# Other PSUM banks for the second product and the third channel block, and one chunk's sums in float32

## The chip, the cores and the metric

The kernel runs on one core of a Trainium2 chip. The metric is the device time of one execution in microseconds (us), the median over the runs shown. Beside it there is one profiled execution, whose trace is read here. The engines are TensorE (PE for matmuls, PEld for the loads of the stationary operand), VectorE (DVE), ScalarE (ACT), GpSimd (POOL) and SyncE (SP, which issues most transfers). Matmuls write to PSUM, which has eight banks of 512 float32 columns on 128 partitions.

## The reference

Two blocks follow one another. The first is a gated linear recurrence over 4 batches, 8 heads, 768 steps and head size 48; the second is a mixture of 8 experts, of which each row takes the best one.

```python
for t in range(S):                                   # recurrence, per batch and head
    state = alpha[:, :, t, :, None] * state + einsum('bhd,bhe->bhde', k[:, :, t], v[:, :, t])
    y[:, :, t] = einsum('bhd,bhde->bhe', q[:, :, t], state)
x = y.transpose(0, 2, 1, 3).reshape(3072, 384)
expert_idx = argmax(x @ w_gate, axis=1)              # w_gate 384 x 8
for e in range(8):                                   # w1[e] 384 x 1024, w2[e] 1024 x 384
    rows = (expert_idx == e)
    out[rows] = gate_w[rows] * (relu(x[rows] @ w1[e]) @ w2[e])
```

gate_w is the softmax weight of the chosen expert. All is float32.

## The kernel before

The instructions of every engine are issued in the order in which the program writes them (a manual schedule); the framework adds the waits that the tiles' readers and writers ask for.

**Recurrence.** The 3072 steps are 24 chunks of 128, taken in the order chunk s = 4 * (time block) + batch. The loop at line 720 runs over i; step i does the scores of chunk i, the transposes of chunk i + 1, the operands of chunk i + 2, the output rows of chunk i - 1 and the running sums of log alpha for chunks up to i + 5 (functions `sums_to` and `new_sums`, lines 619 to 623). A running sum is a matmul of a triangular matrix with the logarithms of 128 steps (`cums`, line 431); ACT then takes two exponentials from the bank `cum` (lines 440 and 441). There are two forms. In the plain one the matmul is float32 (line 434; a float32 product stands in the trace as two loads and two matmuls). In the split one (`apart`, line 411: chunk 7 and chunks from 11 on) ACT makes a float16 copy of the logarithms (line 422), DVE the remainder (`low_part`, line 427), and PE does one float16 and one float32r matmul (lines 436 and 437). The sums of chunks 6 and 7 are both made in step i = 2; chunk 7's is the second, after `attend` and ahead of `keys_values` in PE's order, and its `low_part` stands between the two copies of `transposes` (line 488).

**Experts.** Rows are sorted to eight places by expert size; each place is one group of up to 424, 416, ... 368 rows. 256 rows of place 0 are computed early (`early_layer1` beside the end of the recurrence; `early_layer2`, line 1207, for their second product, in two blocks j = 0 and 1, of which j = 1 is done in two parts with the first product of the other rows of place 0 between them). Places 1 to 7 use a Strassen-like scheme with seven block products (`chain`, line 903; `layer1`, line 952; `layer2`, line 1020): p1 to p7, each in a PSUM bank taken in turn from a pair. Products p1, p3, p5, p6 use pair pA, p4 and p7 pair pB, and p2, the "second product", pair pC. In `layer2` the scheme makes output channels 0 to 255; the third channels (256 to 383) are a plain product of eight float32 matmuls into `d2` (lines 1051 to 1062), whose bank comes from pair pC as well, straight after p2. So p2 of layer 2 writes one bank of pC and `d2` the other. The result of p2 is taken out by a DVE addition into zT (line 924 through the helper at line 192), and `d2` by an ACT copy (line 1064).

**Banks.** `bank(n)` (line 846) hands out the two banks of a pair alternately. pA is the tiles sA and x, pB cum and sB, and tp two tiles of the name tp. pC is the two halves of `y`, which is one tile of two banks: it held outputs and states of the recurrence.

**Turning.** Gathered rows of places 0 and 1 are transposed on PE (`turn`, line 862), block by block of 128 rows, three transposes each; even blocks are copied out by DVE and odd ones by ACT. Place 0 has two blocks here and place 1 four (the last of 32 rows). All four of place 1 alternate between the two tp banks. From place 2 on the transposing is done by transfers (`x_halves`, `x_whole`).

Of the kernel before, what the change touches and what calls it, by code (L numbers as in the profile page):

```python
# [8 lines left out]
F32 = mybir.dt.float32  # L9
# [11 lines left out]
def kernel(  # L21
# [31 lines left out]
    C = 128  # L53
# [180 lines left out]
    g0 = groups[0]  # L234
# [154 lines left out]
    with tc.tile_pool(name="ld", bufs=6) as ld, \  # L389
# [18 lines left out]
            for i in range(many):  # L408
                st[s + i][n] = t[:, i]

        def apart(s):

            return s >= APART or s == 7

        def logs(s):
            t = work.tile([C, Dm], F32, name="lna", bufs=4)
            nc.scalar.activation(t[:], st[s]["a"].rearrange("s h d -> s (h d)"), AF.Ln)
            st[s]["lna"] = t
            if apart(s):

                st[s]["hi"] = work.tile([C, Dm], F16, name="hi", bufs=2)
                nc.scalar.mul(st[s]["hi"][:], t[:], HS)

        def low_part(s):

            t = st[s]["lo"] = work.tile([C, Dm], F32R, name="lo", bufs=1)
            nc.vector.scalar_tensor_tensor(
                t[:], in0=st[s]["hi"][:], scalar=-1.0 / HS, in1=st[s]["lna"][:], op0=ALU.mult, op1=ALU.add,
            )

        def cums(s, bank="cum"):
            cum = ps.tile([C, 512], F32, name="cum", tag=bank)
            if not apart(s):
                nc.tensor.matmul(cum[:, :Dm], lhsT=cum_m[:], rhs=st[s]["lna"][:], start=True, stop=True)
            else:
                nc.tensor.matmul(cum[:, :Dm], lhsT=cum_h[:], rhs=st[s]["hi"][:], start=True, stop=False)
                nc.tensor.matmul(cum[:, :Dm], lhsT=cum_r[:], rhs=st[s]["lo"][:], start=False, stop=True)
            cp = work.tile([C, Dm], F32, name="cp", bufs=6)
            icp = work.tile([C, Dm], F32, name="icp", bufs=6)
            nc.scalar.activation(icp[:], cum[:, :Dm], AF.Exp, scale=-1.0)  # L440
            nc.scalar.activation(cp[:], cum[:, :Dm], AF.Exp)
            st[s]["cp"], st[s]["icp"] = cp, icp
# [42 lines left out]
                    d[e][:].rearrange("s (a p d) -> s a p d", a=2, p=NP), op=ALU.mult,  # L485
                )

        def transposes(s, *lows):
            d = st[s]
            for i, n in enumerate(("kT", "qT")):  # L490
                if i:
                    for t in lows:
                        low_part(t)
                tp = ps.tile([C, NP, C], F32, name="tp", bufs=2)
                for p in range(NP):
                    nc.tensor.transpose(tp[:, p, :], pair(kqb[s % 3][:, i], p), ident[:])  # L496
                d[n] = work.tile([C, NP, C], F32, name=n)

                if 0 < s < B - 1 or i and s < NT - B - 2:
                    nc.vector.tensor_copy(d[n][:], tp[:])  # L500
                else:
                    nc.scalar.copy(d[n][:], tp[:])  # L502
# [217 lines left out]
        for i in range(-4, NT):  # L720
            loads_for(i)
            do(scores, i)
            if i < NT - 1:
                do(result, i - 1)
            do(logits, i - 2)
            if i >= B:
                do(add_state, i - 1)
            do(gate, i - 2)
            if i > 0:
                for s in new_logs(i):  # L730
                    logs(s)
            if 0 < i < NT and i % B == 0:
                decay_cols(i // B)
            do(mask, i, 0)
            do(mask, i, 1)
            if i < B:
                do(add_state, i - 1)
            do(transposes, i + 1, *[s for s in new_sums(i) if apart(s) and s < APART])
            sums = list(new_sums(i))
            for s in sums[:1]:  # L740
                cums(s)
            if i < 0:
                for s in sums[1:]:
                    cums(s, "x")
            do(gate_weight, i - 2)
            route(i)
            for s in new_logs(i):
                if s >= APART:
                    low_part(s)
            do(keep_rows, i - 2)  # L750
            if len(sums) == 1:
                decay_out(sums[0])
            if i == -1:
                for s in range(2):
                    decay_out(s)

            if B - 1 <= i < 2 * B - 1:
                decay_out(i + 1, (1,))
            if i == NT - 2:
                si = next(se)[1]  # L760
                eg["si"] = lambda j, r: si[:r, j : j + 1]
            if i in (B, 2 * B):
                scale_state(i)
            do(operands, i + 2)
            if i > 2 * B and i % B == 0:
                scale_state(i)
            if 0 < i + 1 < NT and (i + 1) % B == 0:
                decay_rows((i + 1) // B)
            elif i >= 0:
                do(scale_state, i + 1)  # L770
            one_hots(nc.gpsimd, *on_gpsimd.get(i, ()))
            do(read_state, i)
            if i == NT - 1:
                early_turn(0)
            do(attend, i)
            if i == NT - 1:
                early_turn(1)
            if i == NT - 2:
                result(i)
            if i >= 0 and sums[1:]:  # L780
                cums(sums[1])
                for s in sums:
                    decay_out(s, (0,) if i else (0, 1))
            do(keys_values, i)
            if i == NT - 3:
                held["tok"] = ps.tile([C, NC], F32, name="tok", tag="cum")
                tokens(held["tok"][:], *range((NG - 1) * TG))
                se = early_gather()
            do(rows, i - 1)
            if i in counts_in:  # L790
                counts(counts_in[i], counted(i - 1))
            if i < 0:
                for s in new_sums(i + 1):
                    logs(s)
            if i == -3:
                second_consts()
            if i in (-4, 0, 1):
                for j in {-4: (0, 1, 2), 0: (3,), 1: (4,)}[i]:
                    late_consts(j)
            if 12 <= i < 22:  # L800
                fetch_part(groups[0], i - 12)
# [38 lines left out]
    xg_pool = ctx.enter_context(tc.tile_pool(name="moe_x", bufs=2))  # L840
    wk = ctx.enter_context(tc.tile_pool(name="moe_wk", bufs=1))

    pairs = dict(pA=("sA", "x"), pB=("cum", "sB"), pC=(0, 1), tp=("tp", "tp"))
    banks = {n: [] for n in pairs}

    def bank(n):
        b = banks[n]
        if len(b) < 2:
            t = pairs[n][len(b)]
            if n == "pC":  # L850
                b.append(y[:, t, :])
            else:
                b.append(ps.tile([C, 512], F32, name=t, bufs=2 if n == "tp" else 1)[:])
        else:
            b.append(b.pop(0))
        return b[-1]
# [2 lines left out]
        return t[:, : DB * C].rearrange("p (a c) -> p a c", a=DB)  # L859


    def turn(g, second="tp"):
        g["xT"] = wk.tile([C, DB, CAP0 + 8], F32, name="xgT")
        for j, r in blocks(g):
            tp = blocks_of(bank(second if j == 1 else "tp"))
            for a in range(DB):
                nc.tensor.transpose(tp[:, a, :r], g["xg"][:r, j, a * C : (a + 1) * C], ident[:r, :r])
            (nc.scalar.copy if j % 2 else nc.vector.tensor_copy)(g["xT"][:, :, j * C : j * C + r], tp[:, :, :r])
            if j == 1:
                yield  # L870
# [336 lines left out]
    def early_layer2(j, fs):  # L1207

        if 0 in fs:
            eg["z"] = bank("tp" if j else "pA")  # L1210
        for f in fs:
            nc.tensor.matmul(
                eg["z"][:, :Dm], lhsT=eg["h"][:, f, j * C : (j + 1) * C], rhs=groups[0]["w2"][:, f, :],
                start=(f == 0), stop=(f == FB - 1),
            )
        if FB - 1 in fs:
            yield
            scatter(eg, j, C, eg["z"][:, :Dm])
        yield
# [35 lines left out]
    gather(groups[1])  # L1255
    next(l2)
    next(early_layer2(1, range(FH)))
    for _ in turn(g0, "pC"):
        pass

    def beside(i):
# [8 lines left out]
    for i, g in enumerate(groups):  # L1270
# [36 lines left out]

        def turned():
            if i == 0:
                for _ in turn(nxt):  # L1310
                    pass
                yield
                row_sums(nxt)
                yield
            z_whole(groups[i - 1], nc.scalar.copy, 0, 1)
            yield
            if nxt:
                row_sums(nxt)
            z_whole(groups[i - 1], nc.scalar.copy, 2)
            z_whole(groups[i - 1], nc.vector.tensor_copy, 3)  # L1320
            yield
            if i + 2 < E:
                for _ in x_halves(groups[i + 2]):
                    pass
            yield
# [25 lines left out]
    with tc.If(nx > 0):  # L1351
        with tc.For_i(0, nx, 1) as i:
# [12 lines left out]
            gi, si = next(d)[:2]  # L1365
            g = dict(n=C, w1=fetch(ex, 1), w2=fetch(ex, 2), gi=lambda j, r: gi[:, 0:1], si=lambda j, r: si[:, 0:1], apart=False)
            gather(g)
            for _ in turn(g):
                pass
            plain(g)  # L1370

# [27 lines left out]
```

## Time and profile before

| | |
|---|---|
| median of 3 runs | 400.71 us (400.21 to 401.31) |
| profiled execution | 401.6 us |
| its span on the core | 399.9 us |
| granted TensorE clock | 0.999 |
| PE busy | 384.2 us, 96% of the span |
| PEld busy | 325.5 us, 81% |
| ACT, DVE, POOL busy | 225.1, 215.4, 147.9 us |

A profile line names an engine, a line of the code, an operation, and the tiles written and read (`y<-h_sb,w` writes y and reads h_sb and w). Where an engine stood idle before an instruction, brackets give for how long and whose end released it. The end of a matmul is modelled, so two consecutive matmuls overlap in the records. The stages of the span are roughly: recurrence to 136 us, place 0 to 177 us, places 1 to 6 to 364 us (some 32 us each), and place 7 to the end.

### The profile page before, as it was taken

The page shows a single profiled execution, that of the slowest core. Times are in us where ns is not written, and L with a number is a line of the kernel's source. Part 1 is how long each engine was busy: PE and PEld are TensorE (multiplying, and loading weights), DVE is VectorE, ACT ScalarE, POOL GpSimd, SP SyncE. Part 2 cuts the span into 40 slices and gives each one's busy share as a digit, 9 for nine tenths or more (in the row PEclk, how much of TensorE's full clock was granted, in tenths as well). Part 3 has the DMA queues.
Part 4 walks back from the last instruction along what each step waited for, and adds up shares of the span by engine and source line. Part 5 has one row for each costly group of instructions (what it writes and reads, how often), then busy time and mean ns, then how long its engine had stood idle before and what let it go on. Part 6 is the DMA issues. An engine that isn't in the chain of part 4 may idle for free.

```text
span 399.9 us, 9108 instructions
## 1 busy us (share of the span) xinstructions
PE 384.2 (96%) x3390; PEld 325.5 (81%) x3390; DVE 215.4 (54%) x652; ACT 225.1 (56%) x516; POOL 147.9 (37%) x203
## 2 busy tenths in 40 slices
PE   7999999999999999999999999999999999999994
PEld 4677888888888886799789879969969969969852
DVE  5554667775666574586833662572591581551200
ACT  4575677776655431125565765665665755763640
POOL 6536564699677105182050034025015012011041
PEclk9999999999999999999999999999999999999999
DMA  8999999999994218769739449758757856701311
GB/s 162 194 185 201 204 216 202 218 222 219 234 227 156 79 41 282 259 177 247 164 93 254 72 195 216 158 179 221 158 190 197 182 179 143 188 6 55 59 57 55
DMA packets 153921, 67.44 MB, mean 169 GB/s; under 512 B 136715, under 2 KB 148098, under 8 KB 153876
## 3 DMA queue, kind: packets, MB, share of 16 engines
q1 hardware_dynamic: 148772, 57.13, 59.7%
q0 software_dynamic: 3408, 9.64, 7.9%
q8 instruction: 27, 0.44, 0.4%
q10 hardware_dynamic: 1696, 0.08, 0.3%
q14 instruction: 18, 0.15, 0.1%
HBM read 49.00 MB, written 9.58 MB: 147 GB/s over the span
## 4 chain that ended last, share of the span: by engine, by line
PE 67%; issue 15%; DMA 4%; ACT 3%; DVE 3%; POOL 3%; SPq 2%; ACTq 1%; POOLq 0%; DVEq 0%
PE y L1055 7%; PE sA L509 4%; PE tp L496 4%; PE y L546 4%; PE x L973 4%; PE sA L973 4%; PE sA L1038 4%; PE x L583 3%; PE y L973 3%; PE cum L973 3%; PE sB L973 3%; PE x L1038 3%; DMA q_sb<-in_q_dram 3%; PE y L536 2%; SPq L405 2%
## 5 line engine op out<-in xcount | busy, mean ns | idle before, releaser
L1085 POOL DMA_INDIRECT out_dram<-zo,sp x25 | 24.8, 991 | 143.2 <-ACT zo L1110 132.2
L1055 PE MATMUL y<-h_sb,w 128*128 128x416 f32 (+5 forms) x96 | 34.5, 502 | 3.7 <-DVE zT L192 3.7
L483 POOL TENSOR_TENSOR kqb<-k_sb,icp 128x384 f32<-128x384 f32 x23 | 23.0, 998 | 30.9 <-DMA k_sb<-in_k_dram 15.9
L1055 PEld LDWEIGHTS y<-h_sb,w 128*128 128x128 f32 x96 | 17.6, 190 | 15.8 <-DVE zT L192 5.5
L509 PE MATMUL sA<-qT,kT 48*128 48x128 f32 x192 | 27.7, 285 | 0.9 <-DVE qT L500 0.9
L509 PE MATMUL sB<-qT,kT 48*128 48x128 f32 x192 | 27.7, 285 | 0.0
L372 POOL DMA_INDIRECT xg<-x_rows,gp x25 | 23.9, 957 | 10.0 <-issue 6.5
L496 PE MATMUL tp<-ident,kqb 128*128 128x128 f32 x192 | 26.2, 280 | 0.2 <-DVE kqb L483 0.2
L509 PEld LDWEIGHTS sA<-qT,kT 48*128 48x128 f32 x192 | 23.1, 187 | 3.8 <-ACT kT L502 1.1
L565 ACT COPY yT<-y 128x512 f32<-128x512 f32 x24 | 14.1, 586 | 19.1 <-PE x L583 9.8
L192 DVE TENSOR_TENSOR h_sb<-cum,u 128x208 f32<-128x208 f32 (+6 forms) x28 | 10.1, 359 | 27.3 <-PE cum L973 20.8
L483 POOL TENSOR_TENSOR kqb<-q_sb,cp 128x384 f32<-128x384 f32 x23 | 23.0, 1001 | 4.1 <-DMA q_sb<-in_q_dram 2.8
L984 ACT ACTIVATE h_sb<-h_sb 128x208 f32<-128x208 f32 (+6 forms) x28 | 10.3, 366 | 25.2 <-DVE h_sb L192 24.4
L192 DVE TENSOR_TENSOR h_sb<-sB,u 128x208 f32<-128x208 f32 (+6 forms) x28 | 10.1, 359 | 26.1 <-PE sB L973 18.7
L496 PEld LDWEIGHTS tp<-ident,kqb 128*128 128x128 f32 x192 | 20.6, 141 | 3.4 <-issue 1.1
L973 PE MATMUL y<-xgT,w 128*128 128x208 f32 (+6 forms) x112 | 23.1, 329 | 0.0
L509 PEld LDWEIGHTS sB<-qT,kT 48*128 48x128 f32 x192 | 23.1, 187 | 0.0
L517 DVE TENSOR_TENSOR dA<-sA,cmask 128x512 f32<-128x512 f32 x24 | 16.5, 687 | 10.1 <-PE sB L509 9.9
L195 DVE TENSOR_TENSOR th<-h_sb,th 128x208 f32<-128x208 f32 (+5 forms) x48 | 17.3, 361 | 7.9 <-ACT h_sb L986 7.9
L583 PE MATMUL x<-iw,yT 128*64 128x104 f32 x368 | 20.8, 255 | 0.3 <-ACT xs L608 0.2
L1110 ACT COPY zo<-zr 128x768 uint16<-128x768 uint16 (+2 forms) x20 | 19.9, 1052 | 0.0
L973 PEld LDWEIGHTS y<-xgT,w 128*128 128x128 f32 x112 | 19.2, 190 | 0.0
(305 smaller groups left out, 1034.0 us busy)
## 6 DMA issues: line engine op xcount, KB each, us to landing
w<-in_moe_w_dram SPq DMA_DIRECT2D x14, 1536.0 KB, 6.4
x_rows<-xs SPq DMA_DIRECT2D x24, 192.0 KB, 3.6
v_sb<-in_v_dram SPq DMA_DIRECT2D x10, 384.0 KB, 5.4
k_sb<-in_k_dram SPq DMA_DIRECT2D x9, 384.0 KB, 6.6
q_sb<-in_q_dram SPq DMA_DIRECT2D x9, 384.0 KB, 5.9
a_sb<-in_alpha_dram SPq DMA_DIRECT2D x7, 384.0 KB, 4.9
a_sb<-in_alpha_dram SPq DMA_DIRECT2D x10, 192.0 KB, 3.8
w<-in_moe_w_dram SPq DMA_DIRECT2D x6, 256.0 KB, 4.0
```

The costliest lines, as they stand in the source:

```text
L192: eng.tensor_tensor(out, a, b, op=ALU.add)
L195: eng.tensor_tensor(out, a, b, op=ALU.subtract)
L372: nc.gpsimd.indirect_dma_start(out=g["xg"][:r, j, :], out_offset=None, in_=x_d[:, :], in_offset=bass.IndirectOffsetOnAxis(ap=g["gi"](j, r) ...
L483: eng.tensor_tensor(by_half(kq[:, i]), d[n].rearrange("s (a p) d -> s a p d", a=2), d[e][:].rearrange("s (a p d) -> s a p d", a=2, p=NP), ...
L496: nc.tensor.transpose(tp[:, p, :], pair(kqb[s % 3][:, i], p), ident[:])
L509: nc.tensor.matmul(t[:, p, :], lhsT=d["kT"][r : r + D, p, :], rhs=d["qT"][r : r + D, p, :], start=True, stop=True,)
L583: nc.tensor.matmul(d["x"][o : o + HC, m, : D2 + E], lhsT=d["yT"][:, m // 2, m % 2, o : o + HC], rhs=iw[:, m, :], start=True, stop=True,)
L973: nc.tensor.matmul(out, lhsT=ops[n_][0], rhs=ops[n_][1], start=first and n_ == names[0], stop=True, skip_group_check=True,)
L1038: nc.tensor.matmul(out, lhsT=lhs, rhs=rhs, start=first and f == 0, stop=True, skip_group_check=True)
L1055: nc.tensor.matmul(d2[:, :n], lhsT=w2[:, f, 2 * C :], rhs=h[:, f, :n], start=(f == 0), stop=(f == FB - 1),)
L1085: ins = nc.gpsimd.indirect_dma_start(out=out[:, :], out_offset=bass.IndirectOffsetOnAxis(ap=g["si"](j, r), axis=0), in_=zo[:r], in_offset= ...
L1110: copy(zo[:r].bitcast(U16).rearrange("p (c h) -> p h c", h=2), g["zr"][:r, j].rearrange("p (h a) c -> p h (a c)", h=2),)
```

## The change

Three edits stand together.

1. pC becomes the two tiles called tp, and the halves of `y` become a pair of their own, named y. All uses of pC (p2 in both layers, `d2`, the first product of place 0, the first row block of place 7) move with it.
2. The early second product of block 1 takes a bank of y in place of tp. `turn` takes a list of pair names, one for each block: place 0's two blocks use pC (tp); place 1's four blocks use pC, pC, y and pB, so four different banks.
3. Chunk 7 is no longer split: its sum is the plain float32 matmul, with no float16 copy on ACT and no remainder on DVE. The extra argument of `transposes` goes.

```diff
-        def apart(s):
-            return s >= APART or s == 7
...
-            if apart(s):
+            if s >= APART:
...
-            if not apart(s):
+            if s < APART:
...
-        def transposes(s, *lows):
+        def transposes(s):
...
-                if i:
-                    for t in lows:
-                        low_part(t)
...
-            do(transposes, i + 1, *[s for s in new_sums(i) if apart(s) and s < APART])
+            do(transposes, i + 1)
...
-    pairs = dict(pA=("sA", "x"), pB=("cum", "sB"), pC=(0, 1), tp=("tp", "tp"))
+    pairs = dict(pA=("sA", "x"), pB=("cum", "sB"), pC=("tp", "tp"), y=(0, 1))
...
-            if n == "pC":
+            if n == "y":
                 b.append(y[:, t, :])
             else:
-                b.append(ps.tile([C, 512], F32, name=t, bufs=2 if n == "tp" else 1)[:])
+                b.append(ps.tile([C, 512], F32, name=t, bufs=2 if t == "tp" else 1)[:])
...
-    def turn(g, second="tp"):
+    def turn(g, *names):
...
-            tp = blocks_of(bank(second if j == 1 else "tp"))
+            tp = blocks_of(bank(names[j]))
...
-            eg["z"] = bank("tp" if j else "pA")
+            eg["z"] = bank("y" if j else "pA")
...
-    for _ in turn(g0, "pC"):
+    for _ in turn(g0, "pC", "pC"):
...
-                for _ in turn(nxt):
+                for _ in turn(nxt, "pC", "pC", "y", "pB"):
...
-            for _ in turn(g):
+            for _ in turn(g, "y"):
```

The last line belongs to a loop over rows beyond a group's capacity. It follows the end of the chain described here and its bank choice changes nothing else.

## The prediction

> **What bounds the kernel now.** I read first the busy times and the shares of the chain that ended last, to learn which engine a saving must come from.
>
> ```profile
> PE 384.2 (96%) x3390; PEld 325.5 (81%) x3390; DVE 215.4 (54%) x652; ACT 225.1 (56%) x516; POOL 147.9 (37%) x203
> ...
> PE 67%; issue 15%; DMA 4%; ACT 3%; DVE 3%; POOL 3%; SPq 2%; ACTq 1%; POOLq 0%; DVEq 0%
> ```
>
> PE is busy all through and carries most of the chain; no other engine reaches 60%. So in the expert stages a PE pause removed should be worth its length, and one added costs its length. The view of waits then names PE's own pauses; the longest in total, on the loads and on the matmuls (columns: total us, times, longest):
>
> ```profile
> PEld y L1055 <- DVE zT L192: 5.5, 6, 1.0
> ...
> PE y L1055 <- DVE zT L192: 3.7, 6, 0.6
> ```
>
> Six times, once in each of places 1 to 6, the third channels (line 1055) wait for a DVE addition into zT. The timeline of place 1 shows which:
>
> ```profile
> 195.78 0.30 PEld L1038 LDWEIGHTS y<-h_sb,w 128*128 128x128 f32 x2 [0.32 <-ACT h_sb L986]
> ...
> 196.62 0.37 DVE L192 TENSOR_TENSOR zT<-y,p 128x208 f32<-128x208 f32 x1
> ...
> 197.04 0.30 PEld L1055 LDWEIGHTS y<-h_sb,w 128*128 128x128 f32 x2 [0.97 <-DVE zT L192]
> 197.04 3.06 PE L1055 MATMUL y<-h_sb,w 128*128 128x416 f32 x8 [0.65 <-DVE zT L192]
> ```
>
> The last loads of p2 start at 195.78; the addition that empties p2's bank ends at 196.99; only then does the first matmul of d2 start. But d2 writes the other bank of pC, last emptied in layer 1 some 6 us earlier, and zT is none of its operands. The one thing both share is the tile y. So the wait is kept by tile, and d2 pays for p2's evacuation.
>
> Place 1's turning is the next PE pause, in the timeline at 167 us:
>
> ```profile
> 167.67 0.48 ACT L1081 COPY zo<-tp 128x384 f32<-128x384 f32 x1 [3.12 <-PE tp L1212]
> ...
> 168.21 0.87 PE L867 MATMUL tp<-ident,xg 128*128 128x128 f32 x6 [0.57 <-ACT zo L1081]
> ...
> 168.86 0.56 DVE L868 COPY xgT<-tp 128x384 f32<-128x384 f32 x1 [3.42 <-PE tp L867]
> ...
> 169.47 0.85 PE L867 MATMUL tp<-ident,xg 128*128 128x128 f32 x6 [0.39 <-DVE xgT L868]
> ...
> 170.25 2.55 PE L1243 MATMUL x<-h_sb,w 128*128 128x168 f32 x16
> ```
>
> Block 0 waits until the early product has left its tp bank (ACT), block 2 until block 0 has left it (DVE). Last, the split sum of chunk 7 against a plain one:
>
> ```profile
> 18.34 0.91 PE L434 MATMUL cum<-lna,cum_m 128*128 128x384 f32 x2
> ...
> 19.18 0.56 PE L557 MATMUL y<-v_sb,kqb 128*48 128x48 f32 x16
> ...
> 23.04 0.52 ACT L422 ACTIVATE hi<-lna 128x384 f16<-128x384 f32 x1
> ...
> 23.59 0.56 DVE L427 SCALAR_TENSOR_TENSOR lo<-hi,lna 128x384 fp32r<-128x384 f16 x1 [0.44 <-ACT hi L422]
> ...
> 24.31 0.49 ACT L441 ACTIVATE cp<-cum 128x384 f32<-128x384 f32 x1
> ...
> 24.86 0.32 PE L436 MATMUL cum<-hi,cum_h 128*128 128x384 f16 x1 [0.57 <-ACT cp L441]
> ...
> 24.88 0.47 PE L437 MATMUL cum<-lo,cum_r 128*128 128x384 f32 x1
> ...
> 25.28 0.56 PE L557 MATMUL y<-v_sb,kqb 128*48 128x48 f32 x16
> ```
>
> From a sum's start to the next product, plain takes 19.18 - 18.34 = 0.84 us of PE, split 25.28 - 24.86 = 0.42. The chain in order of time says what binds there:
>
> ```profile
> 20.18 3.89 DMA k_sb<-in_k_dram
> ...
> 24.71 5.72 DMA q_sb<-in_q_dram
> ```
>
> Loads of k and q, not PE, set the pace until about 31 us.
>
> **What the Trainium skill says.** "PSUM — Partial Sum Buffer", section "PSUM bank collisions raise a hardware error": two engines must be kept apart on one bank, while accesses to different banks run clean. So nothing in the chip orders d2 behind p2's evacuation; the trace's 0.9 us is the program's. "Perfetto Trace Analysis", section "Matmuls", asks for independent matmul groups to rotate through banks so that one's evacuation overlaps the next's matmuls: the trace shows the opposite at 197 us. The same page, "Tensor Engine Instruction (MATMUL, LD_WEIGHTS)", says that a matmul's end is estimated. It fits: the records of consecutive matmuls overlap here, so I size stalls from the starts of loads.
>
> **Part 1, pC as two tiles.** In place 1 p2's last two loads start at 195.78, the second 0.11 later, as after any pause; at 0.176 us per 208-column matmul PE is free for d2 at about 196.24. It got d2's first matmul at about 197.14 (eight at 0.347 plus a tail of 0.18 end at 200.10). That is 0.91 lost, against 0.97 shown on the load row. The total of that row less 0.06 for each restart: 5.5 - 6 x 0.06 = 5.2 us over six places. Nothing takes the wait's place: d2's rhs (blocks 0 to 3 of h) is written by 194.29, w2 landed long before, and with six uses of pC per place d2's new bank was last emptied by layer 1's fourth addition (189.75 + 0.36).
>
> Does the gain stay? Behind d2, p6 needs a DVE difference that ends at 196.14, and would start at 199.03. DVE's sums for the next place end at 203.57 and layer 1 starts at 209.59: 6 us of cover, 5 after the shift. ACT's four xgT copies end at 198.70, ahead of the copy of p6 at 201.60, which moves to 200.7. Weights, gathers and transposes are issued a place ahead (32 us), so 0.9 us each, 5 in all, does not reach them. All else moves with PE. p2 in layer 1 gains nothing: its earlier addition is always done. Place 7 has no d2, and its rows show no such wait. I take -5.2, with 0 and -5.5 as ends.
>
> **Part 2, place 1's turning.** The early product ends on PE at about 167.46 (its record minus the 0.17 overlap). Blocks 0 and 1 go to tp banks last emptied at 164.6, so start at once: 6 transposes at 0.107 = 0.64, to 168.1. Block 2 goes to the second half of y, whose first half the ACT copy of the early product reads until 168.15: by tile it waits until 168.20, 0.1 us. Blocks 2 and 3 then take as now 170.25 - 169.47 = 0.78, and line 1243 starts at 168.98 for 170.25: -1.27. If block 2 need not wait, -1.4; if the earlier start is given back before place 1, 0. Given back means a wait at 177.05, where layer 1 starts: it needs xT (ready before 170), s1 and t1. DVE makes these after the turning copies, so earlier too; its 3.13 us subtraction at 174.04, which runs beside POOL's copies, would be done before POOL's first one at 174.58. Place 0's two blocks wait for their gather as before (0).
>
> **Part 3, chunk 7.** ACT loses 0.52, DVE 0.56, PE gains work of 0.42. The sum waits for the bank cum, freed by ACT's cp (24.80); with ACT 0.5 earlier it starts at 24.34 and lasts 0.84, so keys_values starts at 25.18 for 25.28: -0.1. Behind it stand PE's rows and the next scores, and ACT's exponentials of chunk 7, 0.2 earlier. All is covered by the loads until 31 us. Without that cover it costs at most 0.42. I take 0, ends -0.5 (ACT's lead kept) and +0.42.
>
> **Sum.** -5.2 - 1.27 + 0 = -6.5 on the profiled 401.6 us (span 399.9 plus 1.7 around it): 395.1. The median of the runs lies 0.9 below the profiled one: 400.7 - 6.5 = 394.2.
>
> **Rivals.**
> *The wait isn't by tile.* If d2 waits for another reason, only part 2 is left: 399.4. Against it: six equal waits that end 0.05 us after the addition. Chance 0.06.
> *Given back.* ACT or DVE becomes what PE waits for in places 1 to 6, where PE already waits 0.3 to 0.4 us for ACT copies (line 915). Half of part 1 lost: 396.8. Against it: 5 us of cover. Chance 0.07.
> *Nothing.* As the last, and part 2 lost with part 1: 400.7. Chance 0.03.
> *Slower: the clock.* PE gets busier; a throttle would lower the granted clock. It is 0.999 now; the stretch from 170 to 366 us, about half the run, would have to fall to about 0.97 for PE's 190 us there to lose 6.5. At 0.95 the time is 394.2 + 10 = 404. For it nothing shows. Against it: the clock row is all nines, in slices with PE at 9 too. Chance 0.06.
>
> **How the numbers follow.** The likeliest case (0.78) lies at 394.2, with ends 392.9 to 395.9. The range 392.6 to 397.0 takes in "given back" and leaves out about 2 in 10 with the spread between runs (1.1 us before). Differences below 0.3% (1.2 us) can't be told from none here. Faster is the likeliest case, given back, and most of "not by tile" (1.3 us, on the border): 0.89. Same 0.05, slower 0.06.
>
> **What would show it.** Line 1055 without a wait for zT and its first load within 0.2 us of p2's last; each of places 1 to 6 shorter by 0.9 us; line 867 in place 1 waiting 0.1 us at most, with 1243 about 1.2 us sooner after the early product; the recurrence's end (136 us) unmoved within 0.5. Wrong would be: a new wait of line 1055 or p6, an idle PE at layer 1's start, or the recurrence ending later.

## The result, and the profile after

The changed kernel takes 394.06 us, the median of 4 runs (393.67 to 394.64), against 400.84 us for the kernel before in the same comparison (400.21 to 401.31). The ratio is 0.9833, with a 95% interval of 0.9814 to 0.9852. The forecast was 394.2. The profiled execution took 394.27 us, with a span of 392.5 us and a clock of 0.999.

In the code after the change lines stand some 4 to 7 lower: the third channels are line 1048 (1055 before), turning 860 (867), the second layer's products 1031 (1038), the plain sum 430 (434), and place 0's last product 1236 (1243).

The page's busy times and the shares of the chain, after the change:

```profile
PE 382.1 (97%) x3390; PEld 325.6 (83%) x3390; DVE 211.6 (54%) x651; ACT 225.5 (57%) x515; POOL 149.7 (38%) x203
...
PE 78%; issue 15%; POOL 2%; ACT 2%; DVE 1%; DMA 1%; POOLq 0%; ACTq 0%; DVEq 0%
```

PE has the same 3390 matmuls in 7.4 us less of span. That PE's share of the chain is 78% for 67% is in good part the recurrence: in its first 31 us the chain before holds no work of PE at all, and the chain after is mostly PE (more under part 3 below). The view of waits, for weight loads:

```profile
PEld tp L1048 <- issue: 3.7, 24, 0.2
...
PEld tp L1031 <- ACT h_sb L979: 1.9, 6, 0.3
```

The row with 5.5 us for zT is gone. Of the third channels only the pitch of their loads is left. The largest pause in the second layer is now p2's own, for the last ReLU of h. The timeline of place 1 shows the succession:

```profile
193.44 0.30 PEld L1031 LDWEIGHTS tp<-h_sb,w 128*128 128x128 f32 x2 [0.31 <-ACT h_sb L979]
...
193.72 0.36 PEld L1048 LDWEIGHTS tp<-h_sb,w 128*128 128x128 f32 x2
193.90 2.96 PE L1048 MATMUL tp<-h_sb,w 128*128 128x416 f32 x8
...
194.29 0.37 DVE L192 TENSOR_TENSOR zT<-tp,p 128x208 f32<-128x208 f32 x1
```

The loads of d2 start right behind p2's last two, 0.6 us ahead of the addition that they used to follow. The timeline of place 1's turning:

```profile
166.40 0.82 PE L860 MATMUL tp<-ident,xg 128*128 128x128 f32 x6
...
166.60 0.48 ACT L1074 COPY zo<-y 128x384 f32<-128x384 f32 x1 [3.12 <-PE y L1205]
...
167.13 0.31 PEld L860 LDWEIGHTS y<-ident,xg 128*128 128x128 f32 x3 [0.15 <-ACT zo L1074]
...
167.62 0.37 PE L860 MATMUL sB<-ident,xg 32*128 32x32 f32 x3
...
167.91 2.15 PEld L1236 LDWEIGHTS x<-h_sb,w 128*128 128x128 f32 x15
```

Blocks 0 and 1 run beside the copy of the early product. Block 2, in the other half of y, waits 0.15 us for that copy. And chunk 7's sum, now plain:

```profile
24.26 0.91 PE L430 MATMUL cum<-lna,cum_m 128*128 128x384 f32 x2
...
25.10 0.56 PE L550 MATMUL y<-v_sb,kqb 128*48 128x48 f32 x16
```

It takes 0.84 us to the next product, and that product starts at 25.10 where it started at 25.28. The chain that ended last, in order of time, now runs through this sum:

```profile
24.33 0.84 PE cum L430 x2
25.17 0.49 PE y L550 x16
```

Where the time went is read from starts on PE (us from the span's start; the last column is the difference of the stretch that ends there).

| start of | before | after | stretch |
|---|---|---|---|
| first transposes of place 0 | 156.79 | 155.72 | -1.07 |
| place 0's last product (line 1243 / 1236) | 170.25 | 167.91 | -1.27 |
| place 7's second product, its second layer (line 1124 / 1117) | 377.14 | 369.51 | -5.29 |
| last scatter (POOL) | 395.72 | 388.08 | -0.01 |

The second and third stretch are the two bank edits. I call the two together the expert stretch: 220.35 us before and 213.79 us after, 6.56 less. The first row was not forecast, and is taken up by the first two experiments. The four rows add up to 7.64 us; 0.24 of it is lost again behind the last scatter, so that the span is 7.4 us shorter.

### The profile page after: what moved, and what is told of

Read it like the earlier page. It is cut to its first block, busy times and chain, and to the rows that moved or that the text cites. A ratio compares the mean times of both kernels' runs of the same rounds, so it can differ in the third digit from the quotient of the medians.

```text
span 392.5 us, 9105 instructions
## 1 busy us (share of the span) xinstructions
PE 382.1 (97%) x3390; PEld 325.6 (83%) x3390; DVE 211.6 (54%) x651; ACT 225.5 (57%) x515; POOL 149.7 (38%) x203
## 4 chain that ended last, share of the span: by engine, by line
PE 78%; issue 15%; POOL 2%; ACT 2%; DVE 1%; DMA 1%; POOLq 0%; ACTq 0%; DVEq 0%
PE tp L1048 7%; PE tp L489 6%; PE sA L502 6%; PE y L539 5%; PE x L966 4%; PE sA L966 4%; PE x L576 4%; PE sA L1031 4%; PE tp L966 3%; PE sB L966 3%; PE cum L966 3%; PE x L1031 3%; PE y L529 3%; PE cum L430 2%; PE tp L1031 2%
## 5 line engine op out<-in xcount | busy, mean ns | idle before, releaser
L1078 POOL DMA_INDIRECT out_dram<-zo,sp x25 | 26.1, 1042 | 137.5 <-ACT zo L1103 127.0
L1048 PE MATMUL tp<-h_sb,w 128*128 128x416 f32 (+5 forms) x96 | 33.9, 496 | 0.0
L1048 PEld LDWEIGHTS tp<-h_sb,w 128*128 128x128 f32 x96 | 18.0, 190 | 10.3 <-issue 3.7
L966 PE MATMUL tp<-xgT,w 128*128 128x208 f32 (+6 forms) x112 | 23.1, 329 | 0.0
L966 PEld LDWEIGHTS tp<-xgT,w 128*128 128x128 f32 x112 | 19.3, 190 | 0.0
```

The costliest lines, as they stand in the source:

```text
L966: nc.tensor.matmul(out, lhsT=ops[n_][0], rhs=ops[n_][1], start=first and n_ == names[0], stop=True, skip_group_check=True,)
L1048: nc.tensor.matmul(d2[:, :n], lhsT=w2[:, f, 2 * C :], rhs=h[:, f, :n], start=(f == 0), stop=(f == FB - 1),)
L1078: ins = nc.gpsimd.indirect_dma_start(out=out[:, :], out_offset=bass.IndirectOffsetOnAxis(ap=g["si"](j, r), axis=0), in_=zo[:r], in_offset= ...
```

## The experiments

The theory: the third channels waited because the framework keeps waits by tile and p2 and d2 shared one; turning waited for banks; PE alone sets the expert stretch; the sum is hidden behind loads. Times below are medians; all kernels were timed beside the kernel before (400.5 to 401.1 us).

**Chunk 7's sum alone, in the kernel before.**

```diff
-            return s >= APART or s == 7
+            return s >= APART
```

> The kernel before with edit 3 alone: chunk 7's sum as one plain float32 matmul, banks as before. Theory (the sum is covered by the loads of k and q, and the 1.07 us by which the recurrence ended sooner in the profile after is the scatter of the loads from one execution to the next): 400.8 us, unchanged within 0.4. Rival (ACT's and DVE's lead of 0.5 us in step 2 really shortens the recurrence): 399.8 us, and the output rows of chunk 5 (step 6) start about 1 us sooner than in the kernel before in every such profile.

Measured: 401.07 us against 400.61; ratio 1.0009 (0.9997 to 1.0021). In its profile the first transposes of place 0 start at 155.93, 0.86 sooner than in the profile before, and its expert stretch is 220.37. So the runs show no gain, though its one profile has a shorter recurrence. They would not show a loss of 0.4 us either: the interval reaches to 0.8 us.

**The changed kernel without that sum.** Chunk 7 is split again: all lines of edit 3 are put back, of which this is the first.

```diff
+            return s >= APART or s == 7
```

> The changed kernel with edit 3 undone: chunk 7 is split again, banks as changed. Theory (sum covered): 394.1 us, unchanged within 0.4. Rival (the sum is worth 1.07 us): 395.1 us.

Measured: 394.23 us; expert stretch 213.78, its start at 155.51. The split sum even has the earlier start. Over the eleven profiles of this study (both kernels and the nine experiments) that start lies between 155.43 and 157.61 us, in no order with the form of the sum. The rival falls: the 1.07 us was scatter between executions. In this profile the product behind chunk 7's sum starts at 24.57, so sooner than with the plain sum (25.10); by the fourth start of the row of line 576 after the change (583 here) the two are level, 36.58 against 36.53.

**pC back in the halves of y.**

```diff
-    pairs = dict(pA=("sA", "x"), pB=("cum", "sB"), pC=("tp", "tp"), y=(0, 1))
+    pairs = dict(pA=("sA", "x"), pB=("cum", "sB"), pC=(0, 1), y=("tp", "tp"))
...
-            if n == "y":
+            if n == "pC":
```

> The changed kernel with pair pC in the two halves of y again and the pair named y in the two tp tiles; turning over four banks and chunk 7's sum stay changed. Theory (the wait of the third channels is kept by tile): the wait for the addition into zT is back six times, 5.5 us on the load row, and the time is 394.1 + 5.2 = 399.3 us. Block 2 of place 1 lies in a tile of its own here and need not wait for the early product, so up to 0.1 us less. Rival (the gain came from somewhere else in the change): 394.1 us.

Measured: 401.25 us, 2 us more than expected. Its waits of weight loads show why:

```profile
PEld y L1048 <- DVE zT L192: 5.5, 6, 1.0
...
PEld y L860 <- DVE xgT L861: 1.8, 2, 1.0
```

The six waits are back as expected: from line 1236 to place 7 it takes 206.91 us against 201.60, so 5.31 more. The second row I had overlooked. With pC in y, blocks 0 and 1 of both turnings lie in the two halves of y, and block 1 waits for the copy of block 0. The timeline of place 0:

```profile
155.96 0.56 DVE L861 COPY xgT<-y 128x384 f32<-128x384 f32 x1 [2.44 <-PE y L860]
156.57 0.26 PEld L860 LDWEIGHTS y<-ident,xg 40*128 40x128 f32 x3 [0.89 <-DVE xgT L861]
```

Place 0's turning to line 1220 takes 1.87 us for 1.19, place 1's to line 1236 2.31 for 1.51: 1.48 us together. It is the same wait by tile, in a place where I had not looked for it. In all the expert stretch is 220.61, 6.82 us longer than after the change, where the medians lie 7.2 apart.

**Two banks for place 1's turning.**

```diff
-                for _ in turn(nxt, "pC", "pC", "y", "pB"):
+                for _ in turn(nxt, "pC", "pC", "pC", "pC"):
```

> The changed kernel with place 1's four blocks over the two banks of pC in place of four banks. Blocks 0 and 1 still find their banks free, since the early product stays in y; block 2 waits for the DVE copy of block 0, block 3 for the ACT copy of block 1, which stands behind the copy of the early product. Theory: block 2 starts some 0.4 us later than in the changed kernel, so 394.5 us; most of the 1.27 us of edit 2 comes from taking the early product out of the turning's banks. Rival (the four banks are what counts): 395.3 us.

Measured: 395.79 us (394.42 to 396.48). The expert stretch is 214.18, 0.39 more than after the change, as expected, and all of it in the turning:

```profile
168.82 0.56 DVE L861 COPY xgT<-tp 128x384 f32<-128x384 f32 x1 [2.56 <-PE tp L860]
...
169.43 0.85 PE L860 MATMUL tp<-ident,xg 128*128 128x128 f32 x6 [0.33 <-DVE xgT L861]
```

Block 2 waits for block 0's copy. Of the 1.27 us of edit 2, 0.4 comes from the four banks; the other 0.9 is there with two banks already, so it comes from the early product having left the turning's banks. By the median alone the rival (395.3) would have been the nearer one. But the profiled execution was the slowest of the five (396.48), and what it lost lies ahead of the edit: the first transposes start at 157.61, the latest of all, by instructions that are the same as after the change. On its chain stand two loads of k, of 5.3 us from 28.53 and 5.5 us from 35.67, where the profile after has none. Why they came late is open, and the other four executions have no trace.

**The changed kernel again.**

> The changed kernel itself once more, beside the next ones on one chip. Both theories: 394.1 us; the stretch from the first transpose of place 0 to the first matmul of place 7's second product (213.8 us in its first profile) repeats within 0.1 us, while the recurrence's end scatters by about 1 us from one profile to the next.

Measured: 393.92 us (393.75 to 395.17), ratio 0.9842 (0.9824 to 0.9860); expert stretch 213.77 us.

**p2 in a half of y, d2 in a tp tile.** On top of the experiment with pC in y:

```diff
-            d2 = bank("pC")
+            d2 = bank("y")
```

> As the experiment with pC in the halves of y, but the third channels take their bank from the pair that there holds the two tp tiles: p2 writes a half of y, d2 a tp tile. Theory (the wait comes from p2 and d2 sharing one tile): no wait for zT at the third channels, 5.3 us less than that experiment from line 1236 to place 7; the two extra waits of the turning (block 1 behind block 0, 1.5 us in all) stay, so 394.1 + 1.5 = 395.6 us. Rival (it is the double tile y as such, or anything that reads y late, that makes d2 wait): 401.2 us.

Measured: 396.18 us; expert stretch 215.28, which is 1.49 over the changed kernel, the two turnings. (The median is 0.6 above the expected 395.6; the first transposes start at 156.75 in its profile, 1.03 later than after the change.) Its waits of weight loads:

```profile
PEld tp L1048 <- issue: 3.7, 24, 0.2
...
PEld y L860 <- DVE xgT L861: 1.8, 2, 1.0
```

The wait for zT is gone though p2 stays in the double tile. It takes both in one tile to make d2 wait.

**An extra copy of p2's bank, with pC in two tiles.** One DVE copy more ahead of each addition; the addition overwrites it.

```diff
             terms(new("C"), True, "P2", "R11")
+            if slow:
+                nc.vector.tensor_copy(out(0, 0), at["C"])
...
-        p1, p2, p7, p6, p5, c22, p3, p4 = chain(g, terms, out, res)
+        p1, p2, p7, p6, p5, c22, p3, p4 = chain(g, terms, out, res, True)
```

> The changed kernel with one more DVE copy of p2's bank ahead of the addition into zT in the second layer, six in all, each about 0.36 us. Theory (nothing on PE waits for that addition any more): 394.1 us, unchanged within 0.4. Rival (the addition still sets PE's pace through DVE's later sums): 394.1 + 6 x 0.3 = 395.9 us.

Measured: 394.4 us; expert stretch 213.77. Six added DVE copies cost nothing in that stretch.

**The same copy, with pC in the halves of y.**

> The experiment with pC in the halves of y, with the same extra DVE copy ahead of the addition into zT that cost nothing when pC lay in two tiles. Theory (there the third channels wait for whatever reads p2's half last): each of the six waits grows by the copy, 0.3 us or a little more, so 1.8 to 2.2 us above the 401.25 us of that experiment, 403.2 us; and the stretch from the first transpose of place 0 to place 7's second product grows from 220.6 to 222.5 us. Rival (the wait has a fixed length of its own): 401.25 us.

Measured: 403.81 us; expert stretch 223.03 against 220.61, so 2.42 more. The row of waits and the timeline of place 1:

```profile
PEld y L1050 <- DVE zT L192: 8.0, 6, 1.4
```

```profile
196.42 0.37 DVE L918 COPY zT<-y 128x208 f32<-128x208 f32 x1
196.83 0.38 DVE L192 TENSOR_TENSOR zT<-y,p 128x208 f32<-128x208 f32 x1
...
197.26 0.30 PEld L1050 LDWEIGHTS y<-h_sb,w 128*128 128x128 f32 x2 [1.38 <-DVE zT L192]
```

Each wait grows by 0.41 us, the step from the copy's start to the addition's. I had put 0.3 or a little more, the pitch of DVE operations that don't depend on one another (196.34 and 196.62 in the profile before); this pair, which writes the same place, lies 0.41 apart. So the wait follows whatever reads p2's half last, and the same work beside two tiles is free.

**The third channels ahead of p2.** The waits after the change pointed to p2's pause for the last ReLU.

```diff
-            p2()
             d2 = bank("pC")
...
             third(range(FH))
+            p2()
             p6()
```

> The changed kernel with the first half of the third channels moved ahead of p2 in the second layer of places 1 to 6, so that p2's last two loads no longer wait for the ReLU of the last block of h (0.32 us each, 1.9 us in all). Theory (PE alone sets the time there, and what it stops waiting for is won): 394.1 - 1.9 = 392.2 us. DVE's sums for the next place start 2.8 us later than now and end about 0.5 us before layer 1 needs the last of them. Rival (that cover is too thin, PE waits for DVE at the start of the next place): 394.1 us or more.

Measured: 393.13 us (392.44 to 393.83), ratio to the kernel before 0.9809 (0.9792 to 0.9825). The expert stretch is 212.41 us, 1.36 less than after the change. In the timeline p2 starts well after the ReLU that it used to wait for:

```profile
192.49 2.96 PE L1047 MATMUL tp<-h_sb,w 128*128 128x416 f32 x8
...
193.09 0.55 ACT L979 ACTIVATE h_sb<-h_sb 128x416 f32<-128x416 f32 x1 [0.89 <-DVE h_sb L192]
...
195.28 1.57 PE L1031 MATMUL tp<-h_sb,w 128*128 128x208 f32 x8
```

The 1.9 us expected was the load row's total. Places 1, 2, 3 and 6 shorten by 0.26 to 0.31 us, place 4 by 0.19 and place 5 by 0.07 only. At the end of place 5 PE now waits for DVE. The addition into zT that frees the bank for the last product, first after the change, then here, with the product's loads:

```profile
325.36 0.36 DVE L192 TENSOR_TENSOR zT<-cum,u 128x192 f32<-128x192 f32 x1 [1.56 <-PE cum L1031]
```

```profile
325.08 0.33 DVE L192 TENSOR_TENSOR zT<-cum,u 128x192 f32<-128x192 f32 x1
...
325.47 1.27 PEld L1031 LDWEIGHTS cum<-th,w 128*128 128x128 f32 x8 [0.26 <-DVE zT L192]
```

After the change DVE stood idle for 1.56 us before this addition. Here its sums for the next place start later, it comes to the addition without a pause, and PE waits. In place 4 the loads too start right behind the addition. So the rival came true in part, one product ahead of where I had put it: about 0.3 us of the gain is lost to it (an estimate: what places 4 and 5 lack against the others), and the cover of DVE is used up in these two places. This kernel has the lowest median of all here, 0.8 us below the changed kernel on the same chip. Their timed intervals just overlap, so the trace carries this verdict more than the timed runs do.

## Why the prediction was right

**Part 1, pC as two tiles.** Forecast -5.2 us, measured -5.29. That the wait is kept by tile is shown: it returns when p2 and d2 share y, goes when only d2 leaves, and grows with an added read of p2's half only when they share it. That DVE's addition does not set the stretch as well is shown by the extra copies, 0.4 us more of DVE in each place, which cost nothing. For ACT and POOL no run tests it; that each of places 1 to 6 is 0.86 to 0.91 us shorter says that they took nothing back. It holds for the changed kernel and not much beyond: with the third channels ahead of p2, DVE does stop PE in places 4 and 5. The load row's 5.5 less a small part for each restart was the right size.

**Part 2, turning.** Forecast -1.27, measured -1.27. Block 2's wait by tile for the early product, put at 0.1, is 0.15. That DVE would finish its subtractions ahead of POOL's copies came true: they end at 172.43 and POOL starts at 173.58. The subtraction of 3.13 us is 0.37 now, which is most of DVE's 3.8 us less busy time. It gave PE nothing, since nothing waited for it.

**Part 3, the sum.** Forecast 0, and the runs show none: with the plain sum the median is 0.46 us higher in the kernel before (401.07 to 400.61) and 0.31 lower in the changed one (393.92 to 394.23, on two chips). A cost of a few tenths is not excluded. The reason given, that the loads of k and q cover the sum until 31 us, holds for the profile before but not for most of the others. After the change no load of k or q stands on the chain in the recurrence, and the plain sum does, with 0.84 us; of the nine profiles with the plain sum it does so in seven. In the profile with the chunk split again the remainder on DVE (line 427) stands there in its place, with 0.50 us from 23.05. So the number was right while its reason held in three of the eleven profiles, and that is luck in part. What makes the two forms come out level in such executions is not shown. Locally keys_values starts 0.18 sooner where 0.1 was put, but that isn't the form's doing alone: in the profile before ACT waited 0.58 us for alpha ahead of chunk 7's logarithms.

**The sum.** -6.5 forecast, 6.56 less in the expert stretch, 6.8 between the medians. The profiled execution, forecast at 395.1, came out 0.8 lower: 1.07 less in the recurrence, 0.3 more behind the last scatter and around the span. That the median came within 0.14 us is luck in part, since the four runs of the changed kernel lie up to 1 us apart. The recurrence shows a weak sign among those I had set: "the recurrence's end unmoved within 0.5" can't be read from one profile, since the start of what follows moves by 2 us between executions.

**The rivals.** "Not by tile" fell with the experiments on y, "given back" with the shorter places and the extra copies. The clock stayed at 0.996 to 1.000 in all runs.

## What to carry to other kernels

Where a wait on a PSUM bank names a reader of another bank, look whether both banks are one tile: the view of waits gives the price, and giving the banks to tiles of their own takes it away without moving any work. What a wait on the bounding engine costs is its idle time on the load row less a few hundredths for each restart, as long as the engines behind it have cover. That cover is to be counted in us at every product that needs them, not only at the start of the next place: the wait at the end of place 5 was missed that way. When such a tile is put to another use, look for all pairs of uses that then share it, not only for the one that made the wait.

## What was not expected of the hardware

The time up to the experts scatters by 1.9 us between executions whose instructions up to there are the same: in the five such profiles (the changed kernel twice, two banks for turning, the extra copy with two tiles, the third channels ahead) the first transposes of place 0 start at 155.68 to 157.61 us. By the middle of the recurrence the difference is settled and stays: against the profile before, the changed kernel's lead is 0.97 us at the fourth start of the row of line 583 (576 after), 0.96 to 1.37 at the next three, and 1.04 to 1.07 from the eighth on. The expert stretch of one kernel repeats within 0.02 us (213.79 and 213.77). So a stretch in the trace resolves a tenth of a microsecond where the medians resolve half of one (0.5 us to either side in the interval of the first experiment).
